# A list schedule made by the program orders units 0 to 7, the weight conversion and block 0 on four engines

## The chip, the cores and the metric

The kernel runs on one core of one Trainium2 chip. The metric is the device time of one execution in microseconds (us). A core has a matrix engine (TensorE, PE in the rows), whose weight loads are shown apart (PEld), and VectorE (DVE), ScalarE (ACT), GpSimd (POOL) and SyncE (SP), which here only issues DMA transfers. Each engine runs its own queue in order and waits on semaphores for the others. Matrix products are written to PSUM, of which the kernel uses eight banks of 512 columns; GpSimd can't read PSUM.

## What is computed

Linear attention is followed by a gated feed-forward layer and by a layer of eight experts with routing by the largest logit:

```python
def phi(x):                      # q, k: (4, 8, 576, 64)
    proj = einsum('bhsd,df->bhsf', x, w_phi)
    proj = proj - max(abs(proj), axis=-1)
    return concatenate([exp(proj), exp(-proj)], axis=-1)
kv, z = einsum('bhsf,bhsd->bhfd', phi(k), v), phi(k).sum(2)
attn = einsum('bhsf,bhfd->bhsd', phi(q), kv) / (einsum('bhsf,bhf->bhs', phi(q), z) + 1e-6)
x = attn as (2304, 512)
x = ((silu(x @ w_gate) * (x @ w_val)) @ w_out)        # 512 -> 1536 -> 512
# per token: the expert e of the largest gate logit; out = weights * relu(x @ w1[e]) @ w2[e]
```

## The kernel before

**Units.** The attention is cut into 16 units u of one batch and two heads. A unit has five kinds of steps. `step_qk` (three, c = 0 to 2) projects keys and queries on TensorE, takes a row maximum and subtracts it on VectorE, and makes the key exponentials on ScalarE; the query part is subtracted on VectorE, or for odd units below 8 on ScalarE with a bias. `step_kv` multiplies keys and values, and ScalarE copies the result. `step_tq` (three) transposes the queries, and ScalarE makes their exponentials. `step_num` makes numerator and denominator, and VectorE normalises them into `XT`. `step_tx` (two) transposes the output; ScalarE writes it rounded (`XH`), VectorE the rest (`XL`). Four units make 576 rows of the feed-forward's input.

**Weights.** They come as 64-bit words, 36 pieces (f, w) of 512 columns: column f = 0 to 11, w = gate, value or output weight. For each, SyncE loads a piece into one of three buffers (`conv_load`), ScalarE scales the upper words (L395) and rounds the lower ones (L397), VectorE makes a mask and a shift (L400, L401), GpSimd adds (L404). This is the conversion. Each use of a weight is split into a rounded part (`WH`, ScalarE, L434) and the rest (`WL`, GpSimd, L435), four buffers deep.

**Blocks.** The feed-forward runs over six blocks n of 384 rows. In a block, each column f has two projections of 12 matmuls (`mm_gv`, L444 to L448), a gate (`act_g`, `act_v`: tanh on ScalarE, two products and the rest `GL` on VectorE, L454 to L460), and an output product of 9 matmuls (`mm_o`, L468 to L470) one column later. Block 0 needs units 0 to 3, and it is the one that needs each weight freshly converted. Units 4 to 7 run beside block 0, units 8 to 15 beside blocks 1 to 3.

**What sets the order.** Up to `mark["fixed"]` the program writes TensorE's order out by hand: projections of units 0 and 1, then unit by unit, with some warm-up matmuls (`warmup`, L324) put between. The rest, and the other engines everywhere, are ordered by the framework's scheduler from the order in which the program records them: `run_to` and `conv_to` spread the steps of units 4 to 7 and the conversion evenly over block 0 (`pace`, 36 places), and `hold` keeps conversions from running over two columns ahead. Units in this stretch take turns on PSUM banks 0 to 6, from `mark[PROL - 1]` on banks 5 to 7.

## Time and profile before

| | before |
|---|---|
| median of 3 runs | 955.44 us (955.03 to 956.55) |
| the profiled execution | 956.69 us, span 954.7 us |
| busy PE, PEld | 910.9 us (95%), 791.5 us (83%) |
| busy DVE, ACT, POOL | 625.3 us (65%), 577.3 us (60%), 378.9 us (40%) |
| mean granted TensorE clock | 0.983 of full speed |
| first matmul of block 0, of block 1 | 68.17 us, 201.39 us |

The span runs from the first to the last instruction of the core; the execution's own time is 1.99 us longer. Busy time is the time in which at least one instruction of the engine is in flight. A share over the whole span is an average over stages with different limits, so the stages are read apart.

### The profile page before, as it was taken

Reading aid. Unit: us, or ns where it says so; the run is one execution under the profiler, and the core shown is the slowest. Engines: PE = TensorE matmul, PEld = TensorE weight load, DVE = VectorE, ACT = ScalarE, POOL = GpSimd, SP = SyncE. Lnnn points to the kernel's source line nnn. Section 1 sums busy time; section 2 is a strip of 40 time slices with the busy share of each in tenths; the row PEclk is TensorE's granted clock in tenths of the full one; section 3 lists DMA queues with packets and bytes.
Section 4 is the critical chain, followed back from the end, with each engine's and each line's share of the span. In section 5 each row is a group of like instructions: output and inputs, shape, how many; then the busy total and the mean of one; then the engine's idle time right before and its main releaser. Section 6 shows DMA issues by size and latency. Waiting matters only on the chain.

```text
span 954.7 us, 18339 instructions
## 1 busy us (share of the span) xinstructions
PE 910.9 (95%) x7136; PEld 791.5 (83%) x7136; DVE 625.3 (65%) x1106; ACT 577.3 (60%) x1028; POOL 378.9 (40%) x303
## 2 busy tenths in 40 slices
PE   8789888999999999999999999989999999999995
PEld 5678677799999888888989999979887888878874
DVE  6697787845453743556454543465599988898974
ACT  6876566654435445445545444444588998888873
POOL 1435665644544344434435566556201111112210
PEclk9999899999999999999999999989999999999998
DMA  9663353110001101120000000054001137165230
GB/s 269 170 196 102 126 172 128 46 58 16 1 14 61 26 16 40 26 73 15 1 2 22 14 1 1 34 214 173 34 23 45 45 133 292 40 235 194 98 139 11
DMA packets 20939, 78.88 MB, mean 83 GB/s; under 512 B 5358, under 2 KB 5614, under 8 KB 19056
## 3 DMA queue, kind: packets, MB, share of 16 engines
q1 hardware_dynamic: 17280, 67.60, 21.5%
q0 software_dynamic: 3200, 9.48, 3.0%
q8 instruction: 58, 0.95, 0.4%
q10 hardware_dynamic: 368, 0.59, 0.2%
q14 instruction: 33, 0.27, 0.1%
HBM read 123.23 MB, written 10.00 MB: 140 GB/s over the span
## 4 chain that ended last, share of the span: by engine, by line
PE 72%; issue 4%; DVE 4%; DMA 2%; ACT 1%; POOL 1%; POOLq 0%; DVEq 0%; ACTq 0%
PE banks L444 10%; PE banks L700 9%; PE banks L448 9%; PE banks L447 9%; PE banks L468 5%; PE banks L469 5%; PE banks L470 5%; PE banks L722 3%; PE banks L723 3%; PE banks L724 3%; PE banks L189 2%; PE banks L268 2%; PE banks L236 2%; PE banks L711 1%; DVE arena L483 1%
## 5 line engine op out<-in xcount | busy, mean ns | idle before, releaser
L435 POOL TENSOR_TENSOR arena_r<-arena,arena_r 128x512 fp32r<-128x512 f32 x216 | 284.5, 1319 | 266.9 <-ACT arena_r L434 244.6
L434 ACT ACTIVATE arena_r<-arena 128x512 fp32r<-128x512 f32 x216 | 136.6, 632 | 236.7 <-PE banks L447 146.1
L444 PE MATMUL banks<-arena_r 128*128 128x384 f32 x576 | 202.6, 352 | 0.0
L666 DVE TENSOR_TENSOR arena_r<-arena,arena_r 128x1024 fp32r<-128x1024 f32 x160 | 189.6, 1234 | 19.0 <-ACT arena_r L665 17.8
L448 PE MATMUL banks<-arena_r 128*128 128x384 f32 x576 | 193.7, 336 | 0.0
L447 PE MATMUL banks<-arena_r 128*128 128x384 f32 x576 | 193.4, 336 | 0.0
L665 ACT ACTIVATE arena_r<-arena 128x1024 fp32r<-128x1024 f32 x160 | 161.9, 1066 | 15.5 <-PE banks L700 10.9
L454 DVE SCALAR_TENSOR_TENSOR arena<-arena,banks 128x384 f32<-128x384 f32 x72 | 39.8, 552 | 120.7 <-ACT arena L453 120.4
L700 PE MATMUL banks<-arena_r 128*128 128x512 f32 x480 | 117.8, 398 | 0.0
L444 PEld LDWEIGHTS banks<-arena_r 128*128 128x128 f32 x576 | 108.4, 188 | 5.5 <-DVE arena L454 0.4
L447 PEld LDWEIGHTS banks<-arena_r 128*128 128x128 f32 x576 | 108.6, 189 | 1.2
L728 POOL DMA_INDIRECT out_dram<-arena x20 | 20.8, 1040 | 222.1 <-ACT arena L727 217.4
L448 PEld LDWEIGHTS banks<-arena_r 128*128 128x128 f32 x576 | 108.3, 188 | 0.0
L700 PEld LDWEIGHTS banks<-arena_r 128*128 128x128 f32 x480 | 88.9, 189 | 20.4 <-ACT arena_r L692 2.1
L460 DVE TENSOR_TENSOR arena_r<-arena,arena_r 128x384 fp32r<-128x384 f32 x72 | 70.4, 977 | 38.4 <-ACT arena_r L459 38.1
L468 PE MATMUL banks<-arena_r 128*128 128x512 f32 x216 | 90.5, 419 | 0.0
L469 PE MATMUL banks<-arena_r 128*128 128x512 f32 x216 | 86.9, 402 | 0.0
L470 PE MATMUL banks<-arena_r 128*128 128x512 f32 x216 | 86.6, 402 | 0.0
L722 PE MATMUL banks<-arena_r 128*128 128x512 f32 x160 | 62.7, 392 | 1.0 <-ACT arena_r L665 0.7
L457 DVE TENSOR_TENSOR arena<-arena,banks 128x384 f32<-128x384 f32 x72 | 39.7, 551 | 36.3 <-PE banks L448 36.1
L723 PE MATMUL banks<-arena_r 128*128 128x512 f32 x160 | 62.4, 390 | 0.0
L724 PE MATMUL banks<-arena_r 128*128 128x512 f32 x160 | 62.4, 390 | 0.0
(124 smaller groups left out, 1391.3 us busy)
## 6 DMA issues: line engine op xcount, KB each, us to landing
arena<-mw SPq DMA_DIRECT2D x40, 2048.0 KB
ov_conv<-w1cat SPq DMA_DIRECT2D x24, 512.0 KB
arena<-w1cat SPq DMA_DIRECT2D x12, 512.0 KB
arena<-v SPq DMA_DIRECT2D x16, 325.0 KB
x2d<-arena SPq DMA_DIRECT2D x18, 256.0 KB
arena<-qT SPq DMA_DIRECT2D x15, 288.0 KB
arena<-kT SPq DMA_DIRECT2D x15, 288.0 KB
ov_gather<-x2d,arena POOLq DMA_INDIRECT x20, 3.5
```

Source lines behind the costliest of these rows:

```text
L434: ACT.activation(wh, wr, AF.Copy)
L435: POOL.tensor_tensor(out=wl, in0=wr, in1=wh.bitcast(F32), op=ALU.subtract)
L444: mm = PE.matmul(ps, wh[:, c], xh, start=(k == 0), stop=False)
L447: PE.matmul(ps, wh[:, c], xl, start=False, stop=False)
L448: PE.matmul(ps, wl[:, c], xh, start=False, stop=(k == 3))
L468: PE.matmul(ps, GH[f % 2][:, ts_], woh, start=(f == 0), stop=False)
L469: PE.matmul(ps, GH[f % 2][:, ts_], wol, start=False, stop=False)
L470: PE.matmul(ps, GL[f % 2][:, ts_], woh, start=False, stop=(f == NFT - 1))
L665: ACT.activation(h, src, AF.Copy)
L666: DVE.tensor_tensor(out=l, in0=src, in1=h.bitcast(F32), op=ALU.subtract)
L700: PE.matmul(PS[:, HB[h], :], lhs, w[:, h * 512:(h + 1) * 512], start=a, stop=b)
L722: PE.matmul(ps, HTH[:, k, :], wh[:, cs], start=(k == 0), stop=False)
```

## The change

A class `Plan` takes operations with an engine, a duration in us, a due time and what they read and write. Its `run` simulates four engines (SyncE and the transfers as further ones) while the program is built: again and again it takes, of the operations whose inputs are done, the one that can start first, and among those of that engine which could start at the same time the one that is due first; it gives out PSUM banks, and calls the operation's function, so that the instructions are recorded in that order. `first_part` puts units 0 to 7, unit 8's projections, the 36 conversions, the splits and block 0 into it. The steps are cut into the part of each engine for that (`qk_mm`, `k_sub`, `k_exp`, `q_sub`, and so on). Where TensorE would stand idle for over 0.9 us in the plan before its time 56, `filler` puts warm-up matmuls. The order so made is fixed for PE, DVE, ACT and POOL.

Besides, the rounding of the first `NRP` = 8 pieces moves from ScalarE to GpSimd, the subtraction `g_lo` of block 0 from VectorE to GpSimd, the second output transpose is of 128 rows instead of 64 in its last part, and `hold` goes. Blocks 1 to 5 and units 8 to 15 are recorded as before.

```diff
-PRE = 9
 PROL = 4
-AHEAD = 2
+NRP = 8
 WARM = 11
...
+class Plan:
+    LAT = 0.15
+    def __init__(self):
+        self.ops, self.last_w, self.readers = [], {}, {}
+    def op(self, eng, dur, due, fn, reads=(), writes=(), banks=0, pool=(), holder=None):
+        i = len(self.ops)
+        deps = set()
+        for r in reads:
+            if r in self.last_w:
+                deps.add(self.last_w[r])
+            self.readers.setdefault(r, []).append(i)
+        for w in writes:
+            if w in self.last_w:
+                deps.add(self.last_w[w])
+            deps.update(self.readers.pop(w, ()))
+            self.last_w[w] = i
+        deps.discard(i)
+        if banks:
+            holder = {"users": 0, "end": 0.0, "owner": i}
+        elif holder is not None:
+            deps.add(holder["owner"])
+            holder["users"] += 1
+        self.ops.append(dict(eng=eng, dur=dur, due=due, fn=fn, deps=deps, banks=banks, pool=pool, holder=holder))
+        return holder
+    def run(self, filler):
+        ops = self.ops
+        left = [len(o["deps"]) for o in ops]
+        after = [[] for _ in ops]
+        for i, o in enumerate(ops):
+            for d in o["deps"]:
+                after[d].append(i)
+        end = [0.0] * len(ops)
+        free = {}
+        bank_free = [0.0] * 8
+        ready = {i for i, n in enumerate(left) if n == 0}
+        while ready:
+            best = None
+            for i in ready:
+                o = ops[i]
+                t = max([free.get(o["eng"], 0.0)] + [end[d] + self.LAT * (ops[d]["eng"] != o["eng"]) for d in o["deps"]])
+                if o["banks"]:
+                    b = sorted((bank_free[b], b) for b in o["pool"])[:o["banks"]]
+                    if b[-1][0] == float("inf"):
+                        continue
+                    t = max(t, b[-1][0] + self.LAT)
+                    o["take"] = [x[1] for x in b]
+                cand = (t, o["due"], i)
+                o["at"] = t
+                if best is None or cand < best:
+                    best = cand
+            assert best is not None, "no op can be taken"
+            same = [(ops[i]["due"], i) for i in ready if ops[i]["eng"] == ops[best[2]]["eng"]
+                    and ops[i].get("at", 1e9) <= best[0] + 0.05 and (not ops[i]["banks"] or all(
+                        bank_free[b] < float("inf") for b in ops[i].get("take", ())))]
+            i = min(same)[1]
+            o = ops[i]
+            ready.discard(i)
+            filler(o["eng"], free.get(o["eng"], 0.0), o["at"])
+            if o["banks"]:
+                o["holder"]["ps"] = [b for b in o["take"]]
+                for b in o["take"]:
+                    bank_free[b] = float("inf")
+                o["fn"](*o["take"])
+            elif o["holder"] is not None:
+                o["fn"](*o["holder"]["ps"])
+            else:
+                o["fn"]()
+            end[i] = o["at"] + o["dur"]
+            free[o["eng"]] = end[i]
+            h = o["holder"]
+            if h is not None and not o["banks"]:
+                h["users"] -= 1
+                h["end"] = max(h["end"], end[i])
+                if h["users"] == 0:
+                    for b in h["ps"]:
+                        bank_free[b] = h["end"]
+            for j in after[i]:
+                left[j] -= 1
+                if left[j] == 0:
+                    ready.add(j)
+        assert not any(left)
+        return free
...
-    for x in qk(0) + qk(1):
-        add(*x)
-    add(warmup, 6)
-    for u in range(PROL):
-        add(step_kv, u)
-        if u >= 2:
-            tx(u - 2)
-        for c in range(3):
-            add(step_tq, u, c)
-        if u:
-            add(step_num, u - 1)
-        add(warmup, 2)
-        for x in qk(u + 2) if u + 2 < PROL else []:
-            add(*x)
-    for x in qk(PROL):
-        add(*x)
-    tx(PROL - 2)
-    add(step_num, PROL - 1)
-    mark["fixed"] = len(steps)
-    tx(PROL - 1)
-    for u in range(PROL, 16):
-        if u == QSW:
-            add(step_ov)
+            PE.matmul(PS[:, 4, :], warm[:, 0:P], warm, start=True, stop=True)
+    add(step_ov)
+    for u in range(QSW, 16):
...
-        at = seen.get(i // 3 - AHEAD)
-        if at is not None:
-            tc.add_manual_dep(ins.ins, at.name, mybir.DependencyInfo(
-                mybir.DependencyClass.NoSync, mybir.DependencyReason.SCHED_ONLY), reason="pace of the weights")
...
+    def conv_round(i):
+        lo = ST[i % 3].rearrange("p (n two) -> p n two", two=2)[:, :, 0].bitcast(U32)
+        r = CP[i % 2].bitcast(I32)
+        if i < NRP:
+            POOL.tensor_scalar(out=r, in0=lo, scalar1=2.0 ** -29, scalar2=None, op0=ALU.mult)
+        else:
+            ACT.activation(r, lo, AF.Copy, scale=2.0 ** -29)
...
+    def g_lo(f, eng=DVE):
+        eng.tensor_tensor(out=GL[f % 2], in0=GP, in1=GH[f % 2].bitcast(F32), op=ALU.subtract)
...
+    def first_part():
+        pl = Plan()
+        op = pl.op
+        def unit(u, qkd, kvd, numd, txd):
+            z, early = two(u), u < PROL
+            sub = u % 2 == 0
+            banks = (0, 1, 2, 3, 5, 6, 7) if u < 3 else (0, 1, 2, 5, 6, 7) if u == 3 else (5, 6, 7)
+            for c in range(3):
+                d = qkd + 1.2 * c
+                h = op("PE", 0.8, d, lambda bq, bk, c=c: qk_mm(u, c, bq, bk), [("x", u)], [("qk", u, c), ("xr", u % 2)], 2, banks)
+                op("DVE", 1.1, d + 1, lambda bq, bk, c=c: k_sub(u, c, bk), [("qk", u, c)], [("kp", z, c)], holder=h)
+                op("ACT", 1.08, d + 2, lambda c=c: k_exp(u, c), [], [("kp", z, c)])
+                if sub:
+                    op("DVE", 1.1, d + 2, lambda bq, bk, c=c: q_sub(u, c, bq), [("qk", u, c)], [("tq", z, c)], holder=h)
+                else:
+                    op("DVE", 0.55, d + 2, lambda bq, bk, c=c: amax(bq, MQ[c]), [("qk", u, c)], [("m", c)], holder=h)
+                    op("ACT", 1.11, d + 3, lambda bq, bk, c=c: q_bias(u, c, bq), [("m", c)], [("tq", z, c)], holder=h)
+            if u >= 8:
+                return
+            h = op("PE", 2.2, kvd, lambda b: kv_mm(u, b), [("kp", z, c) for c in range(3)] + [("v", u)],
+                   [("kvm", u)], 1, banks)
+            op("ACT", 0.41, kvd + 1, lambda b: kv_copy(u, b), [("kvm", u)], [("kv", u % 2)], holder=h)
+            for c in range(3):
+                h = op("PE", 0.4, kvd + 1 + c, lambda b, c=c: tq_mm(u, c, b), [("tq", z, c)], [("tqm", u, c)], 1, banks)
+                op("ACT", 1.07, kvd + 2 + c, lambda b, c=c: tq_exp(u, c, b), [("tqm", u, c)], [("qp", z, c)], holder=h)
+            h = op("PE", 2.2, numd, lambda b0, b1: num_mm(u, b0, b1), [("qp", z, c) for c in range(3)] + [("kv", u % 2)],
+                   [("num", u)], 2, banks)
+            op("DVE", 1.36, numd + 1, lambda b0, b1: normalise(0, b0), [("num", u)], [("xt", 0), ("xt", 1)], holder=h)
+            op("DVE", 1.0, numd + 1.5, lambda b0, b1: normalise(1, b1), [("num", u)], [("xt", 0), ("xt", 1)], holder=h)
+            for part in range(2):
+                n = len(x_pieces(u, part))
+                js = sorted({x[1] for x in x_pieces(u, part)})
+                h = op("PE", 0.45, txd + part, lambda b, part=part: tx_mm(u, part, b), [("xt", part)],
+                       [("txm", u, part)], 1, banks)
+                op("ACT", 0.38 * n, txd + part + 0.5, lambda b, part=part: x_hi(u, part, b), [("txm", u, part)],
+                   [("xh", j, u) for j in js], holder=h)
+                op("DVE", 0.42 * n, txd + part + 0.7, lambda b, part=part: x_lo(u, part, b),
+                   [("txm", u, part)] + [("xh", j, u) for j in js], [("xl", j, u) for j in js], holder=h)
+        start = {("x", 0): 7.0, ("x", 1): 10.5, ("v", 0): 12.5, ("v", 1): 16.0, ("x", 2): 17.0, ("x", 3): 21.0}
+        start.update({("v", u): 0.0 for u in range(2, 8)})
+        for name, t in start.items():
+            op(("at",) + name, t, t, lambda: None, [], [name])
+        for u in range(4):
+            b = 7 + 11 * u
+            unit(u, b, b + 8, b + 13, b + 17)
+        B0, PER = 56.0, 9.6
+        for u in range(4, 9):
+            b = 48 + 28 * (u - 4)
+            unit(u, b, b + 10, b + 16, b + 21)
+        for i in range(3 * NFT):
+            f, w = divmod(i, 3)
+            due = B0 + PER * f + (0, 2, 6)[w] - 14
+            if i >= 3:
+                op("SP", 0.1, due - 8, lambda i=i: conv_load(i), [], [("st", i % 3)])
+                op(("dma", i), 4.0, due - 8, lambda: None, [], [("st", i % 3)])
+            else:
+                op(("dma", i), 14.0 + 3 * i, due - 8, lambda: None, [], [("st", i % 3)])
+            op("ACT", 0.69, due, lambda i=i: conv_scale(i), [("st", i % 3)], [("cu", i % 2)])
+            op("POOL" if i < NRP else "ACT", 1.65 if i < NRP else 0.69, due + 0.5, lambda i=i: conv_round(i), [("st", i % 3)], [("cp", i % 2)])
+            op("DVE", 1.75, due + 1, lambda i=i: conv_bits(i), [("cu", i % 2)], [("wr", i)])
+            op("POOL", 1.37, due + 3, lambda i=i: conv_add(i), [("cp", i % 2)], [("wr", i)])
+        last = where[1, 0, 0] + 2
+        def cut_weights(i):
+            n, f, w = uses[i]
+            due = B0 + PER * (12 * n + f + (1 if w == 2 else 0)) + (0, 3, 6)[w] - 5
+            op("ACT", 0.64, due, lambda: split_hi(i), [("wr", 3 * f + w)], [("wh", i % 4)])
+            op("POOL", 1.37, due + 1, lambda: split_lo(i), [("wh", i % 4), ("wr", 3 * f + w)], [("wl", i % 4)])
+        for i in range(3):
+            cut_weights(i)
+        for i in range(where[1, 0, 0]):
+            n, f, w = uses[i]
+            at = B0 + PER * (f + (1 if w == 2 else 0)) + (0, 3, 6)[w]
+            wts = [("wh", i % 4), ("wl", i % 4)]
+            xs = [(x, 0, u) for x in ("xh", "xl") for u in range(4)]
+            if w == 2:
+                op("PE", 2.1, at, lambda f=f: o_mm(0, f), wts + [("gh", f % 2), ("gl", f % 2)], [("out",)])
+            elif w == 0:
+                op("PE", 2.2, at, lambda f=f: gv_mm(0, f, 0), wts + xs, [("G",)])
+                op("ACT", 0.49, at + 1, g_tanh, [("G",)], [("ts",)])
+                op("DVE", 0.55, at + 1.5, g_mul, [("ts",), ("G",)], [("gp",)])
+            else:
+                op("PE", 2.2, at, lambda f=f: gv_mm(0, f, 1), wts + xs, [("V",)])
+                op("DVE", 0.55, at + 1, v_mul, [("V",)], [("gp",)])
+                op("ACT", 0.53, at + 1.5, lambda f=f: g_hi(f), [("gp",)], [("gh", f % 2)])
+                op("POOL", 1.05, at + 2, lambda f=f: g_lo(f, POOL), [("gp",), ("gh", f % 2)], [("gl", f % 2)])
+            cut_weights(i + 3)
+        def filler(eng, t0, t1):
+            if eng == "PE" and t1 < B0 and t1 - t0 > 0.9:
+                warmup(int((t1 - t0 - 0.3) / 0.4))
+        ET = mybir.EngineType
+        with tc.manual_schedule(engines={ET.PE, ET.DVE, ET.Activation, ET.Pool}):
+            ends = pl.run(filler)
...
-    with tc.manual_schedule(engines={mybir.EngineType.PE}):
-        for i in range(mark["fixed"]):
-            run_to(i + 1)
-            conv_to(PRE * 3 * i // mark["fixed"])
-    run_to(mark[PROL - 1])
+    POOL.memset(XT[64:P, 4, :], 0.0)
+    first_part()
     state["banks"] = [5, 6, 7]
-    need = {0: mark[7], 1: mark[8] - 2, 2: mark[11], 3: mark[15], 4: 0, 5: 0}
-    for i in range(3):
-        split(i)
-    prev = None
+    need = {1: mark[8] - 2, 2: mark[11], 3: mark[15], 4: 0, 5: 0}
+    prev = (0, NFT - 1)
```

**What moves, on TensorE at the start.** In both orders the rows below are the steps of unit 0 behind its projections (128x512 is a warm-up; 64x130 and 64x65 are kv; 128x128 x9 or x3 query transposes). Before, ahead of them stand 11 warm-ups, the 36 projections of units 0 and 1, and 6 warm-ups:

```order
L227 MATMUL banks<-arena 64x130 x4
L236 MATMUL banks<-arena 64x65 x32
L248 MATMUL banks<-arena 128x128 x9
L324 LDWEIGHTS arena
L324 MATMUL banks<-arena 128x512
```

After, ahead of the rows below stand 28 warm-ups; the first row with x18 is unit 0's projections, the rows with x6 are unit 1's:

```order
L459 MATMUL banks<-arena 128x512
L286 MATMUL banks<-arena 128x128 x18
L365 MATMUL banks<-arena 128x128 x3
L286 MATMUL banks<-arena 128x128 x6
L459 LDWEIGHTS arena
```

The transposes of unit 0 have moved ahead of unit 1's projections, one chunk at a time. Before block 0 there are 20 more warm-ups in eight places, where there were 14.

**On VectorE around the first gate of block 0.** Before (L400 and L401 are a conversion, L454, L457 and L460 the gate, L310 is `XL` of unit 3):

```order
L400 TENSOR_SCALAR arena<-arena 128x512
L310 TENSOR_TENSOR arena_r<-banks,arena_r 128x384
L310 TENSOR_TENSOR arena_r<-banks,arena_r 128x192
L401 SCALAR_TENSOR_TENSOR arena<-arena 128x512
L400 TENSOR_SCALAR arena<-arena 128x512
L454 SCALAR_TENSOR_TENSOR arena<-arena,banks 128x384
L401 SCALAR_TENSOR_TENSOR arena<-arena 128x512
L457 TENSOR_TENSOR arena<-arena,banks 128x384
L460 TENSOR_TENSOR arena_r<-arena,arena_r 128x384
```

After (L504 and L505 are the conversion, L552 and L555 the gate, L440 is `XL`):

```order
L440 TENSOR_TENSOR arena_r<-banks,arena_r 128x384
L440 TENSOR_TENSOR arena_r<-banks,arena_r 128x192
L504 TENSOR_SCALAR arena<-arena 128x512
L505 SCALAR_TENSOR_TENSOR arena<-arena 128x512
L504 TENSOR_SCALAR arena<-arena 128x512
L505 SCALAR_TENSOR_TENSOR arena<-arena 128x512
L552 SCALAR_TENSOR_TENSOR arena<-arena,banks 128x384
L504 TENSOR_SCALAR arena<-arena 128x512
L505 SCALAR_TENSOR_TENSOR arena<-arena 128x512
L555 TENSOR_TENSOR arena<-arena,banks 128x384
```

The third operation of the gate has left VectorE, and the conversions stand whole. Six conversions stand before unit 3's last `XL`, 30 behind it; 12 had been done by 68 us before.

**On GpSimd at the same place.** Before (L404 adds of the conversion, L435 splits):

```order
L435 TENSOR_TENSOR arena_r<-arena,arena_r 128x512 x3
L404 TENSOR_TENSOR arena<-arena,ov_conv 128x512
L435 TENSOR_TENSOR arena_r<-arena,arena_r 128x512
L404 TENSOR_TENSOR arena<-arena 128x512
L435 TENSOR_TENSOR arena_r<-arena,arena_r 128x512
```

After (L509 adds, L526 splits, L498 the last rounding on GpSimd, L561 `g_lo` of columns 0 and 1):

```order
L498 TENSOR_SCALAR arena<-ov_conv 128x512
L509 TENSOR_TENSOR arena<-arena,ov_conv 128x512
L509 TENSOR_TENSOR arena<-arena 128x512
L526 TENSOR_TENSOR arena_r<-arena,arena_r 128x512
L509 TENSOR_TENSOR arena<-arena,ov_conv 128x512
L561 TENSOR_TENSOR arena_r<-arena,arena_r 128x384
L526 TENSOR_TENSOR arena_r<-arena,arena_r 128x512
L509 TENSOR_TENSOR arena<-arena 128x512
L526 TENSOR_TENSOR arena_r<-arena,arena_r 128x512
L561 TENSOR_TENSOR arena_r<-arena,arena_r 128x384
```

Eight roundings now stand on GpSimd ahead of block 0, and from there on a `g_lo` in each column among the adds and splits.

## Rows read from the trace of the kernel before

**Rows 1.** Windows: us, busy PE, PEld, DVE, ACT, POOL, PEclk, DMA share, GB/s.

```profile
0.00:68.17 68.17, 56.23 (x920) 44.47 (x920) 52.78 (x121) 50.77 (x119) 20.62 (x23) 0.95 0.75 218
68.17:201.39 133.22, 119.31 (x1083) 103.18 (x1082) 101.69 (x175) 83.97 (x183) 79.72 (x59) 0.96 0.36 109
201.39:300.00 98.61, 98.61 (x765) 90.02 (x765) 45.58 (x93) 46.51 (x92) 51.61 (x40) 1.00 0.08 26
```

**Rows 2.** TensorE's waits up to 200 us: us in total, times, longest.

```profile
PE banks L189 <- DVE arena L207: 5.2, 4, 2.9
```

**Rows 3.** Timeline of PE: start, us, line, operation, shapes, count; idle before.

```profile
1.20 4.88 PE L324 MATMUL banks<-arena 128*128 128x512 bf16 x11 [1.20 <-DVE arena L771]
6.00 3.05 PE L189 MATMUL banks<-arena 64*128 64x128 f32 x38
...
20.60 0.59 PE L324 MATMUL banks<-arena 128*128 128x512 bf16 x2
21.12 2.28 PE L189 MATMUL banks<-arena 64*128 64x128 f32 x36
...
26.92 1.15 PE L268 MATMUL banks<-arena 128*64 128x65 f32 x32
...
29.38 0.60 PE L324 MATMUL banks<-arena 128*128 128x512 bf16 x2
...
49.06 0.55 PE L297 MATMUL banks<-arena 128*128 128x128 f32 x3
...
49.85 1.20 PE L248 MATMUL banks<-arena 128*128 128x128 f32 x9
```

**Rows 4.** Timeline of PE where block 1 starts.

```profile
201.39 0.44 PE L444 MATMUL banks<-arena_r 128*128 128x384 f32 x1
...
205.68 0.39 PE L468 MATMUL banks<-arena_r 128*128 128x512 f32 x1
...
207.75 0.60 PE L499 MATMUL banks<-arena 128*128 128x128 f32 x4
```

**Rows 5.** Timeline of DVE at the start.

```profile
7.53 1.02 DVE L197 TENSOR_REDUCE arena<-banks 128x3 f32<-128x384 f32 x2 [6.39 <-PE banks L189]
...
9.40 1.01 DVE L197 TENSOR_REDUCE arena<-banks 128x3 f32<-128x384 f32 x2
```

**Rows 6.** DVE by line up to 206 us: count | busy us, mean ns | idle before.

```profile
L401 DVE SCALAR_TENSOR_TENSOR arena<-arena 128x512 int32<-128x512 int32 x36 | 34.5, 959 | 0.9
L400 DVE TENSOR_SCALAR arena<-arena 128x512 int32<-128x512 int32 x36 | 29.0, 805 | 6.2 <-ACT arena L395 4.7
...
L460 DVE TENSOR_TENSOR arena_r<-arena,arena_r 128x384 fp32r<-128x384 f32 x12 | 11.2, 932 | 12.1 <-ACT arena_r L459 12.0
...
L310 DVE TENSOR_TENSOR arena_r<-banks,arena_r 128x192 fp32r<-128x192 f32 x16 | 5.5, 352 | 2.4 <-ACT arena_r L309 2.3
...
L310 DVE TENSOR_TENSOR arena_r<-banks,arena_r 128x384 fp32r<-128x384 f32 x4 | 2.2, 556 | 1.8 <-ACT arena_r L309 1.8
```

**Rows 7.** Timeline of DVE, the normalisation of unit 5.

```profile
121.10 0.17 DVE L276 TENSOR_SCALAR arena<-banks 128x6 f32<-128x6 f32 x1 [2.65 <-PE banks L265]
...
122.75 0.86 DVE L280 TENSOR_TENSOR arena<-banks,arena 64x256 f32<-64x256 f32 x2
```

**Rows 8.** Timeline of DVE, two conversions.

```profile
123.84 0.43 DVE L400 TENSOR_SCALAR arena<-arena 128x512 int32<-128x512 int32 x1 [0.23 <-ACT arena L395]
124.30 0.69 DVE L401 SCALAR_TENSOR_TENSOR arena<-arena 128x512 int32<-128x512 int32 x1
125.10 1.56 DVE L400 TENSOR_SCALAR arena<-arena 128x512 int32<-128x512 int32 x1
126.69 1.66 DVE L401 SCALAR_TENSOR_TENSOR arena<-arena 128x512 int32<-128x512 int32 x1
```

**Rows 9.** Timeline of POOL in the same us.

```profile
125.07 1.30 POOL L404 TENSOR_TENSOR arena<-arena 128x512 int32<-128x512 int32 x1 [2.51 <-DVE arena L401]
126.32 1.48 POOL L435 TENSOR_TENSOR arena_r<-arena,arena_r 128x512 fp32r<-128x512 f32 x1
```

249 lines of the change are left out of this document (132 added, 117 removed).

## Prediction

> **What bounds the kernel now.** The busy time by stage comes first, because the share over the whole span (TensorE 95%) hides where it is lost. From the first matmul of block 1 at 201.39 us on [rows 4], TensorE is busy for 98.61 of 98.61 us; before that it has two stages with holes: 56.23 busy of 68.17 us up to the first matmul of block 0, and 119.31 of 133.22 us in block 0 [rows 1]. I call them stage A and stage B. Since TensorE has no idle time behind 201.39, what the first part saves reaches the end one to one, and the change touches the first part alone. So the question is: when does block 1 start after the change?
>
> The view of waits says what the holes are: TensorE waits for VectorE and ScalarE to hand over the small steps of a unit, 5.2 us in four waits for a `q_sub` alone [rows 2]. No engine is full over both stages: VectorE is busy for 52.78 + 101.69 us, ScalarE 50.77 + 83.97, GpSimd 20.62 + 79.72 of 201.39 [rows 1]. TensorE's 119.31 busy us in stage B also contain work at the lower clock, whose granted mean there is 0.96 [rows 1].
>
> **How much TensorE must do.** In an undisturbed run of instructions a unit's projections, kv, query transposes and num steps take from 21.12 to 29.38 us, 8.26 us, and its output transposes 49.06 to 49.85, 0.79 us: 9.05 us a unit; without num and output transposes 5.8 us (21.12 to 26.92) [rows 3]. A weight column f costs 4.29 us for its two projections (201.39 to 205.68) and 2.07 us for its output product (205.68 to 207.75) [rows 4].
>
> **The change, part by part, stage A.** The list of TensorE's order has 28 warm-up matmuls ahead of the first unit where there were 11, and 20 more before block 0 where there were 14. The 11 take from 1.20 to 6.00 us, 0.44 us each; the two behind unit 0 go at 0.26 us (20.60 to 21.12) [rows 3]. The 17 new ones cost 4.4 us at the one pace and 7.5 at the other; I take 5.1 (the first four at the slow pace), because data of unit 0 are there by 6.00. So the projections start at 11.1 us, and VectorE, which starts at 7.53 now [rows 5], at 12.6.
>
> VectorE then has, up to the last `x_lo` of unit 3: 54 maxima and subtractions, at 0.47 us each (four from 7.53 to 9.40, [rows 5]) 25.4 us; six weight conversions at 0.805 + 0.959 = 1.76 us, 10.6 us [rows 6] (the old order has 12 by then); four normalisations of 2.5 us (121.10 to 123.61, [rows 7]), 10.0 us; four `x_lo` of 0.96 us (7.7 us for eight units, [rows 6]), 3.9 us. That is 49.9 us, and 62.5 us is the earliest end. TensorE's own work up to there is four units at 9.05, 5.8 for the fifth and 20 fillers at 0.26: 47.2 us, end at 58.3. So VectorE leads stage A. Today it is busy for 52.78 of the 60.6 us from 7.53 to 68.17, 87%; at that rate the stage would end at 69.9. I take 64: the list hands each engine its steps one at a time and interleaved, the three transposes of a query chunk right behind its subtraction, and 1.76 us already contains waits.
>
> **Stage B.** TensorE: twelve columns at 4.29 and eleven output products at 2.07 us (the twelfth lies in block 1 in both orders), 74.3 us; num and output transposes of unit 4, 3.25; units 5 to 7, 27.2; one of unit 8's three projection steps, 0.76. Sum 105.4 us. Two steps of unit 8, 1.5 us, slip behind the start of block 1; today none does. VectorE: 30 conversions at 1.76, 52.8; 24 gate products at 0.47, 11.3; 34 maxima and subtractions, 16.0; four normalisations and `x_lo`, 13.9: 94.0 us. Its twelve `g_lo` (932 ns, [rows 6]) go to GpSimd, and eight of ScalarE's roundings of weights with them, in stage A; ScalarE only gets lighter and had 49 us free in stage B [rows 1].
>
> GpSimd is where the price is. The rows at 125 us show a DVE conversion and a GpSimd operation that exclude each other: the mask of a conversion takes 0.43 and its shift 0.69 us alone (123.84, 124.30), but 1.56 and 1.66 us against GpSimd operations [rows 8], each ending 0.29 and 0.55 us after GpSimd's at 126.37 and 127.80 [rows 9]. VectorE's operations on PSUM are not stretched: `x_lo` of 384 columns has a mean of 0.556 us [rows 6]. So the two queues share one resource. In stage B it has to carry 27 conversion adds and 32 splits at 1.25 us (125.07 to 126.32), 73.8 us; eleven `g_lo` on GpSimd, which no row shows: 0.94 us by the length, 384 of 512 columns, 10.3 us (bounds: 0.56 us, a subtraction of this size on VectorE, and 1.5, a held GpSimd operation; 6 to 16 us in all); and 30 conversions at 0.29 + 0.55, 25.2 us, or 33.6 at the lengths they have alone. Sum 109.3 to 117.7 us: more than TensorE's 105.4, and no list that leaves this resource out can see it. The eight roundings on GpSimd are not in the trace either; between 1.25 and 2.5 us (twice the other operation) they are 10 to 20 us of stage A, where GpSimd is idle for 47.5 of 68.17 us, so they cost nothing unless they delay a conversion.
>
> The Trainium skill says the same of the resource (GPSIMD Engine Reference, Key points): GpSimd shares its SBUF interfaces with VectorE, and contends with DVE instructions in a two-port mode or with two SBUF inputs; the rows agree (1.66 against 0.69 us). Its section Engine selection speaks against `g_lo` on GpSimd: two-input elementwise work is about twice as slow there; as an estimate by that, 1.1 us each and 1.8 us more over the eleven.
>
> Stage B lies between 109.3 us (the shared resource never idle) and the 133.2 of today. I take 120, near the middle: the resource would then be used for 91% of the stage, VectorE for 78% (76% today) and TensorE for 88% at the full pace, against 105.4 / 133.2 = 79% today.
>
> **The sum.** Block 1 starts at 64 + 120 = 184 us in place of 201.39; less the 1.5 us that slip, 15.9 us are saved. The profiled execution took 956.69 us for a span of 954.70; its span should become about 938.8. The median of the runs is 955.44, 1.25 below that execution; 15.9 less gives 939.5 us.
>
> **Rivals.** *The list is kept nearly as planned.* Nothing waits but for the shared resource: block 1 at 62.5 + 109.3 = 171.8, saved 28.1, 927.3 us; with TensorE alone as the bound 167.9 and 923.4 us. For it: VectorE reached 87% in stage A already. Against it: the exclusion, which stretches both queues when both are busy. Chance 0.15.
>
> *Little is gained.* The late start stays (stage A ends at 69.9, VectorE at 87%), and stage B takes 126 us, since each of four fixed orders waits for the others where they run late: block 1 at 195.9, saved 4.0, 951.4 us. For it: with fixed orders on four engines one late step holds everything behind it, a `split_hi` on ScalarE that waits for TensorE to free a weight buffer, for example. Chance 0.13; another 0.06 that it comes out within 0.2%.
>
> *The alternation of VectorE and GpSimd, slower.* With GpSimd's queue never empty, every conversion meets an operation there twice and takes 1.56 + 1.66 = 3.22 us, as at 125.10 [rows 8]. 30 times 1.46 us more makes 137.8 us of VectorE's 94.0; filled to 97%, stage B takes 142 us, block 1 starts at 206, and the kernel takes 955.44 + 4.6 + 1.5 = 961.5 us. It decides from 3.02 us a conversion on (131.8 us of VectorE in 135.9). Against it: GpSimd is busy for 84 of 120 us, not always, and many DVE operations lie between two conversions. Chance 0.08.
>
> **Numbers.** The forecast (932 to 948 us) has 0.58, the four others 0.15, 0.13, 0.06 and 0.08. About 0.2%, 1.9 us, is what a measurement of this kernel can tell from no change. Faster: 0.58 + 0.15 + 0.13 = 0.86; within: 0.06; slower: 0.08. The range must reach into the first two rivals: 927 leaves out the part of the first that TensorE alone bounds, 953 the last two cases; together about 0.2.
>
> **What the profile after would show.** First projection near 11 us; first matmul of block 0 near 64; first of block 1 near 184; TensorE full behind it as now. The mean of mask and shift together should be 1.7 to 2.2 us; above 3 the third rival is right, below 1.5 the exclusion was overrated. `g_lo` on GpSimd near 0.94 us. If TensorE's idle time in stage B is under 5 us, the first rival holds; if block 0 starts after 68, stage A was misjudged, and the warm-ups or VectorE's waits say why. The prediction is wrong if TensorE behind block 1 shows holes it has not now, since the whole argument rests on there being none.

## The result, and the profile after

| | before | after |
|---|---|---|
| median (range) | 956.00 us (955.03 to 958.07) | 945.78 us (945.33 to 946.96) |
| ratio, 95% interval | | 0.9892 [0.9873, 0.9912] |
| the profiled execution, its span | 956.69, 954.7 us | 945.33, 943.6 us |
| first projection | 6.00 us | 9.04 us |
| first matmul of block 0 (stage A) | 68.17 us | 64.31 us |
| first matmul of block 1 | 201.39 us | 190.73 us |
| block 0 (stage B) | 133.22 us | 126.42 us |

The kernel became 10.2 us faster. Block 1 starts 10.66 us earlier and the span is 11.1 us shorter, so the first part alone made the difference, nearly one to one. The forecast had 15.9 us.

The three windows of the kernel after answer to [rows 1] (us, then busy PE, PEld, DVE, ACT, POOL with instructions, PEclk, DMA share, GB/s):

```profile
0.00:64.31 64.31, 58.44 (x942) 45.54 (x942) 48.10 (x109) 42.97 (x101) 23.29 (x25) 0.97 0.64 182
64.31:190.73 126.42, 114.56 (x1063) 99.60 (x1062) 110.14 (x166) 89.78 (x190) 103.19 (x79) 0.97 0.47 136
190.73:290.00 99.27, 98.85 (x736) 89.62 (x737) 50.51 (x102) 47.64 (x95) 50.25 (x39) 1.00 0.09 27
```

Stage A came out at 64.31 us. From block 1 on TensorE is nearly full (98.85 of 99.27 us), as it was before. Stage B is 6.4 us longer than the 120 forecast. In it TensorE is idle for 11.86 us, but no engine is full over the whole stage: VectorE has 87%, GpSimd 82%, with 79 instructions where it had 59.

The waits of TensorE in stage B (us in total, times, longest) answer to [rows 2]:

```profile
PE banks L542 <- POOL arena_r L526: 4.5, 3, 3.0
PE banks L286 <- DVE arena_r L440: 2.5, 2, 2.1
PE banks L422 <- DVE arena L407: 2.3, 1, 2.3
PE banks L540 <- DVE arena L552: 1.0, 1, 1.0
PE banks L365 <- DVE arena L309: 0.7, 1, 0.7
```

L542 is the part of a column's projections that uses `WL`, and L526 the split that makes it; L440 writes `x_lo`, L407 is the normalisation, L309 a `q_sub`. TensorE now waits for GpSimd and VectorE, in few and long waits, and one short one is for a `q_sub`.

Before, the subtraction of a query was the largest cause of its waits: 7.7 us up to 200 us for a `q_sub` on VectorE (L207, 5.2 us in [rows 2] and the 2.5 below), and 9.6 us for the same step with a bias on ScalarE (L205):

```profile
PE banks L189 <- ACT arena L205: 3.5, 1, 3.5
...
PE banks L300 <- DVE arena L207: 2.5, 2, 1.6
PE banks L297 <- ACT arena L205: 2.4, 1, 2.4
PE banks L300 <- ACT arena L205: 2.2, 2, 1.2
...
PE banks L248 <- ACT arena L205: 1.5, 2, 0.7
```

Of these 17.3 us, the kernel after has 4.5 left: the 0.7 in stage B, and in stage A

```profile
PE banks L365 <- DVE arena L309: 2.5, 4, 1.2
PE banks L286 <- ACT arena L314: 1.3, 1, 1.3
```

By line, the mask (L504) and the shift (L505) of the conversion in stage B answer to [rows 6] (busy us, mean ns, idle before):

```profile
L505 DVE SCALAR_TENSOR_TENSOR arena<-arena 128x512 int32<-128x512 int32 x31 | 40.7, 1313 | 1.1
L504 DVE TENSOR_SCALAR arena<-arena 128x512 int32<-128x512 int32 x30 | 29.9, 998 | 3.2 <-ACT arena L491 2.4
```

Together 2.31 us a conversion, against the 1.76 taken. That 1.76 is a mean over both stages of the kernel before. In its stage B alone, where GpSimd was busy for 60%, the two took 1.93 us, and in its stage A 1.41 (485 and 927 ns):

```profile
L401 DVE SCALAR_TENSOR_TENSOR arena<-arena 128x512 int32<-128x512 int32 x25 | 24.1, 964 | 0.6
L400 DVE TENSOR_SCALAR arena<-arena 128x512 int32<-128x512 int32 x24 | 23.2, 965 | 4.4 <-ACT arena L395 3.3
```

In stage A of the kernel after, where GpSimd is busy for 23.29 of 64.31 us, they take 0.91 and 0.52 us:

```profile
L505 DVE SCALAR_TENSOR_TENSOR arena<-arena 128x512 int32<-128x512 int32 x6 | 5.5, 911 | 0.2
...
L504 DVE TENSOR_SCALAR arena<-arena 128x512 int32<-128x512 int32 x6 | 3.1, 517 | 0.1
```

GpSimd's own lines in stage B, splits (L526) and the moved `g_lo` (L561):

```profile
L526 POOL TENSOR_TENSOR arena_r<-arena,arena_r 128x512 fp32r<-128x512 f32 x35 | 49.5, 1420 | 5.2 <-ACT arena_r L522 4.0 <-issue 1.2
...
L561 POOL TENSOR_TENSOR arena_r<-arena,arena_r 128x384 fp32r<-128x384 f32 x12 | 14.3, 1189 | 2.1 <-ACT arena_r L558 2.1
```

What stretches the conversion is seen in six us of the timelines of VectorE and GpSimd (start, us); they answer to [rows 8, 9]:

```profile
136.69 1.55 DVE L504 TENSOR_SCALAR arena<-arena 128x512 int32<-128x512 int32 x1
138.27 1.39 DVE L505 SCALAR_TENSOR_TENSOR arena<-arena 128x512 int32<-128x512 int32 x1
139.58 0.55 DVE L294 TENSOR_REDUCE arena<-banks 128x3 f32<-128x384 f32 x1
140.04 1.32 DVE L504 TENSOR_SCALAR arena<-arena 128x512 int32<-128x512 int32 x1
141.40 1.68 DVE L505 SCALAR_TENSOR_TENSOR arena<-arena 128x512 int32<-128x512 int32 x1
```

```profile
136.66 1.29 POOL L509 TENSOR_TENSOR arena<-arena,ov_conv 128x512 int32<-128x512 int32 x1 [0.63 <-DVE arena L505]
137.91 1.20 POOL L561 TENSOR_TENSOR arena_r<-arena,arena_r 128x384 fp32r<-128x384 f32 x1
139.80 1.28 POOL L509 TENSOR_TENSOR arena<-arena 128x512 int32<-128x512 int32 x1 [0.69 <-DVE arena L505]
141.04 1.49 POOL L526 TENSOR_TENSOR arena_r<-arena,arena_r 128x512 fp32r<-128x512 f32 x1
```

The mask at 136.69 starts 0.03 us behind an add and ends at 138.24, 0.29 us after it (137.95); the shift at 138.27 starts inside the `g_lo` that ends at 139.11 and ends 0.55 us after it. Alone they take 0.43 and 0.69 us. The reduction from PSUM at 139.58 takes its usual 0.55.

### The profile page after: what moved, and what is told of

The parts are those of the page before. It is cut to its first block, busy times and chain, and to the rows that moved or that the text cites. A ratio compares the mean times of both kernels' runs of the same rounds, so it can differ in the third digit from the quotient of the medians.

```text
span 943.6 us, 18408 instructions
## 1 busy us (share of the span) xinstructions
PE 908.5 (96%) x7159; PEld 790.2 (84%) x7159; DVE 640.8 (68%) x1094; ACT 578.2 (61%) x1020; POOL 404.6 (43%) x324
## 4 chain that ended last, share of the span: by engine, by line
PE 76%; DVE 15%; issue 4%; DMA 3%; ACT 2%; POOL 0%; POOLq 0%; DVEq 0%; ACTq 0%
PE banks L915 10%; PE banks L540 10%; PE banks L542 9%; PE banks L541 9%; PE banks L578 5%; PE banks L579 5%; PE banks L580 5%; PE banks L286 3%; DVE arena L505 3%; PE banks L937 3%; PE banks L938 3%; PE banks L939 3%; DVE arena L504 2%; PE banks L347 2%; PE banks L390 2%
## 5 line engine op out<-in xcount | busy, mean ns | idle before, releaser
L526 POOL TENSOR_TENSOR arena_r<-arena,arena_r 128x512 fp32r<-128x512 f32 x216 | 285.8, 1325 | 247.2 <-ACT arena_r L522 234.4
L542 PE MATMUL banks<-arena_r 128*128 128x384 f32 x576 | 193.9, 337 | 4.5 <-POOL arena_r L526 4.5
L915 PE MATMUL banks<-arena_r 128*128 128x512 f32 x480 | 116.8, 396 | 0.0
L540 PEld LDWEIGHTS banks<-arena_r 128*128 128x128 f32 x576 | 108.3, 188 | 7.8 <-issue 1.4
L542 PEld LDWEIGHTS banks<-arena_r 128*128 128x128 f32 x576 | 108.1, 188 | 5.8 <-POOL arena_r L526 5.8
L552 DVE SCALAR_TENSOR_TENSOR arena<-arena,banks 128x384 f32<-128x384 f32 x72 | 39.7, 552 | 107.6 <-ACT arena L549 107.5
L578 PE MATMUL banks<-arena_r 128*128 128x512 f32 x216 | 90.0, 417 | 0.0
L579 PE MATMUL banks<-arena_r 128*128 128x512 f32 x216 | 86.6, 401 | 0.0
L580 PE MATMUL banks<-arena_r 128*128 128x512 f32 x216 | 86.5, 402 | 0.0
L561 DVE TENSOR_TENSOR arena_r<-arena,arena_r 128x384 fp32r<-128x384 f32 x60 | 60.9, 1015 | 27.7 <-ACT arena_r L558 27.5
L294 DVE TENSOR_REDUCE arena<-banks 128x3 f32<-128x384 f32 x96 | 52.7, 554 | 23.6 <-PE banks L286 21.5
L555 DVE TENSOR_TENSOR arena<-arena,banks 128x384 f32<-128x384 f32 x72 | 39.8, 552 | 39.6 <-PE banks L542 38.8
L937 PE MATMUL banks<-arena_r 128*128 128x512 f32 x160 | 62.7, 392 | 1.0 <-ACT arena_r L880 0.7
L939 PE MATMUL banks<-arena_r 128*128 128x512 f32 x160 | 62.4, 390 | 0.0
```

The lines of the kernel that those rows point to most:

```text
L526: POOL.tensor_tensor(out=WL[i % 4], in0=WR[f][w], in1=WH[i % 4].bitcast(F32), op=ALU.subtract)
L540: PE.matmul(ps, wh[:, c], xh, start=(k == 0), stop=False)
L542: PE.matmul(ps, wl[:, c], xh, start=False, stop=(k == 3))
L578: PE.matmul(ps, GH[f % 2][:, ts_], woh, start=(f == 0), stop=False)
L579: PE.matmul(ps, GH[f % 2][:, ts_], wol, start=False, stop=False)
L580: PE.matmul(ps, GL[f % 2][:, ts_], woh, start=False, stop=(f == NFT - 1))
```

## The experiments

The first theory after the result was **VectorE alone**: its work in stage B, 94.0 us by the forecast, grew by 30 x 0.55 = 16.5 to 110.5, and it shows 110.14. The rivals were **the shared resource** of the prediction (GpSimd's operations and VectorE's conversions exclude each other, so their sum counts), and that the order itself leaves holes. Stage A ends at the first matmul of block 0, stage B at that of block 1. Where a run gives an operation another engine, length or due time in the plan, the program makes its list anew, so the order of the whole first part differs too: this is so in e1, e5, e6, e7, e8 and e10. e3, e4 and e11 keep the order of the kernel after on VectorE, ScalarE and GpSimd.

**Which part of the change gains.** e7 keeps the planner and puts `g_lo` and the roundings back; e9 keeps the old order and moves only these two to GpSimd.

```diff
 e7_order_only, against the kernel after
-NRP = 8
+NRP = 0
-op("POOL", 1.05, at + 2, lambda f=f: g_lo(f, POOL), ...
+op("DVE", 0.98, at + 2, lambda f=f: g_lo(f), ...
 e9_place_only, against the kernel before
-            ACT.activation(ri, st[:, :, 0].bitcast(U32), AF.Copy, scale=2.0 ** -29)
+            if i < 8:
+                POOL.tensor_scalar(out=ri, in0=..., scalar1=2.0 ** -29, scalar2=None, op0=ALU.mult)
+            else: ACT.activation(...)
-        DVE.tensor_tensor(out=GL[f % 2], ...)
+        (POOL if n == 0 else DVE).tensor_tensor(out=GL[f % 2], ...)
```

Expected of e7: 

> The list's order without the two moves: g_lo on VectorE and all roundings on ScalarE. Theory now (the resource that GpSimd and VectorE's two conversion operations share is the bound of stage B, not VectorE alone): the roundings lie in stage A, where GpSimd is idle for 41 of 64 us, so nothing changes against the run with g_lo alone moved back: 937 to 941 us. Rival (ScalarE needs the relief in stage A): stage A 3 to 5 us longer, 942 to 944 us.

Expected of e9: 

> The old order and the old scheduler with the two moves alone: g_lo of block 0 and the first eight roundings on GpSimd. If the moves are worth something by themselves (11 us of VectorE and 5.5 of ScalarE less): 948 to 952 us. Theory (the moves only load the shared resource, which the old order does not fill): 954 to 958 us. If an output product waits for g_lo behind other work on GpSimd: over 959 us.

| | old placement | `g_lo`, roundings on GpSimd |
|---|---|---|
| old order | 955.93 us | e9: 957.52 us, 1.0016 [1.0002, 1.0029] |
| new order | e7: 941.09 us, 0.9835 [0.9817, 0.9854] | after: 945.78 us, 0.9892 [0.9873, 0.9912] |

The order gains 11.7 to 14.8 us, and the two placements together cost 1.6 us in the old order and 4.7 in the new one. (The small changes beside the order, the transpose of 128 rows and the missing `hold`, are in e7 too and were not tried apart.) Stages A and B of e7 are 72.12 and 118.11 us, of e9 71.80 and 134.83. e9 came out as the theory had it. e7 did not: against e1 below, which has only `g_lo` put back, its stage A is 7.8 us longer, as its rival said and by more, and its stage B 3.4 us shorter, with two conversions fewer (28 for 30). The stage A of e7 also has more matmuls (1009 for 941) and a lower granted clock (0.91 for 0.97), so why it is longer stays open. All the same, the roundings on GpSimd show no cost: with them block 1 starts 4.4 us earlier (185.81 for 190.24), and the median is 2.2 us lower, though the ranges overlap. By these runs the loss of the placements is `g_lo`'s.

**What `g_lo` on GpSimd costs.** e1 is the kernel after with `g_lo` alone back on VectorE (its second `-`/`+` pair above). Expected: 

> Undoes one part: g_lo of block 0 is back on VectorE, in the plan with 0.98 us. Theory (exclusion: stage B is 126.4 us in place of 120 because a conversion on VectorE meets GpSimd operations and takes 2.31 us in place of 1.76): VectorE, 87% busy in stage B and 96% from 110 to 170 us, gets 11 operations of about 1.1 us, and its 60 conversion operations wait some 4 us less; stage B 6 to 8 us longer, 951 to 954 us. Rival (the four fixed orders wait for each other, and no engine is the bound): 944 to 948 us.

Measured: 938.85 us, 0.9828 [0.9807, 0.9848], below both ranges. Stage A is unchanged (64.34). The window of stage B and, in it, VectorE's lines:

```profile
64.34:185.81 121.47, 113.75 (x1076) 99.08 (x1074) 112.96 (x185) 91.39 (x193) 88.32 (x66) 0.99 0.48 141
```

```profile
L505 DVE SCALAR_TENSOR_TENSOR arena<-arena 128x512 int32<-128x512 int32 x31 | 35.4, 1141 | 1.1
L504 DVE TENSOR_SCALAR arena<-arena 128x512 int32<-128x512 int32 x30 | 27.0, 901 | 3.1 <-ACT arena L491 3.0
...
L561 DVE TENSOR_TENSOR arena_r<-arena,arena_r 128x384 fp32r<-128x384 f32 x12 | 9.9, 826 | 0.0
```

VectorE got twelve more operations and is busier (112.96 us of 121.47), and the stage is 4.95 us shorter. That fells the theory that VectorE's own work is the bound. The conversion fell from 2.31 to 2.04 us, which pays 8.1 of the 9.9 us that `g_lo` takes there. How much of the 4.95 us is the place of `g_lo` and how much the new list, this run can't tell; e11 below keeps the list.

**How little of GpSimd's work must stay for the holes to close.** In e3 GpSimd's operations of the first part work on 32 columns in place of 512 or 384; the rest of the low parts of weights and gates is left out. With that the routing is another and the expert layer runs more slots, so its total, 1011.64 us (1.0581 [1.0557, 1.0605]), is not to be compared; stages A and B issue the same instructions.

```diff
-        POOL.tensor_tensor(out=WL[i % 4], in0=WR[f][w], ...)
+        POOL.tensor_tensor(out=WL[i % 4][:, 0:c], in0=WR[f][w][:, 0:c], ...)
 (c = 32; and so for the rounding, the add and g_lo)
```

Expected: 

> Leaves out 15 of 16 columns (11 of 12 for g_lo) of every GpSimd operation in stages A and B, so that most of the low parts of the weights stay unset; all instructions, waits and orders stay. Theory (exclusion): mask and shift take 1.15 us together in place of 2.31, VectorE in stage B falls from 110 us to about 75, and TensorE's own 105 us are the bound: stage B 106 to 112 us, 926 to 932 us in all. Rival (fixed orders waiting for each other): TensorE's waits stay, 942 to 946 us; between them, 933 to 941, both have a share.

The window of stage B, and its two lines of the conversion:

```profile
63.65:171.79 108.14, 108.09 (x1063) 97.06 (x1061) 75.76 (x165) 88.02 (x190) 22.59 (x78) 1.00 0.52 157
```

```profile
L505 DVE SCALAR_TENSOR_TENSOR arena<-arena 128x512 int32<-128x512 int32 x30 | 20.9, 696 | 1.0
L504 DVE TENSOR_SCALAR arena<-arena 128x512 int32<-128x512 int32 x30 | 13.1, 437 | 7.3 <-ACT arena L491 6.6
```

The same order, with nearly the same number of instructions on every engine, leaves TensorE no wait at all: 108.09 busy of 108.14 us, at the full clock. So the order has no holes of its own, and TensorE's work in stage B is 108.1 us (105.4 forecast). The conversion takes 1.13 us, the sum of its lengths alone (0.43 and 0.69). VectorE's list of operations is the same, only GpSimd's operations are shorter: this shows that what GpSimd does is what stretches the conversion.

**`g_lo` where it is, but short.** e11 cuts only `g_lo` to 32 columns, on GpSimd, at its place; the low part of block 0's gates is zero in the other 352. It tells the hold of a `g_lo` from its place in the queue.

```diff
-        eng.tensor_tensor(out=GL[f % 2], in0=GP, ...)
+        c = 32 if eng is POOL else BT
+        eng.tensor_tensor(out=GL[f % 2][:, 0:c], in0=GP[:, 0:c], ...)
```

Expected: 

> The changed kernel with the g_lo of block 0 left on GpSimd, at the same place of its queue, but 32 columns wide instead of 384; this leaves out 352 columns of the low part of the gates of block 0, which is zero there. It measures what g_lo holds of the resource that GpSimd and VectorE share. Shared-resource theory: a g_lo shrinks from 1.19 to about 0.3 us, twelve of them give back 8 to 11 us, stage B takes 115 to 119 us (e1, where VectorE has them at half the hold, 121.5), and the mean of mask and shift falls below 2.1 us together. Rival, the hand-over: what e1 gained is g_lo's place (late on GpSimd, behind splits, with the output product behind it): then the thin g_lo in the same place keeps most of the loss, stage B 124 to 126.5. Rival, length only: g_lo is only shorter by 0.9 us on a queue that is not full, and stage B gains as much as the waits of TensorE on GpSimd end (4.5 us of waits on a split): 122 us. The total may be read only if blocks 1 to 5 keep their length; the stages decide.

Measured: 942.20 us, 0.9854 [0.9834, 0.9875]; its stage A is 1.7 us longer than after's (the first projection starts at 10.10 us for 9.04). Window of stage B and lines:

```profile
66.01:187.63 121.62, 112.67 (x1063) 98.61 (x1062) 104.14 (x166) 89.30 (x190) 93.94 (x79) 0.99 0.49 142
```

```profile
L505 DVE SCALAR_TENSOR_TENSOR arena<-arena 128x512 int32<-128x512 int32 x31 | 34.4, 1108 | 1.1
L504 DVE TENSOR_SCALAR arena<-arena 128x512 int32<-128x512 int32 x30 | 30.4, 1015 | 3.9 <-ACT arena L491 3.1
```

```profile
L562 POOL TENSOR_TENSOR arena_r<-arena,arena_r 128x32 fp32r<-128x32 f32 x12 | 6.0, 499 | 2.2 <-ACT arena_r L558 2.2
```

The place alone, the hand-over rival, falls: stage B is 4.8 us shorter with `g_lo` in its old place. But the shared resource had 115 to 119 us, and 121.62 is what the third rival (length on GpSimd) had. A thin `g_lo` takes 0.50 us, not 0.3, and gives back 12 x 0.69 = 8.3 us, of which the stage shows 4.8. So the sum of the resource has the sign right, and near TensorE's 108 us it no longer gives its size. This run can't tell which of the two queues a `g_lo` held back.

**A plan that knows the exclusion.** In e6 the simulated queues of GpSimd and of the conversions exclude each other, with the lengths that the operations have alone; the work is the same.

```diff
+                if o["excl"]:
+                    t = max(t, port)
...
+            if o["excl"]:
+                port = end[i]
-            op("DVE", 1.75, due + 1, lambda i=i: conv_bits(i), ...
+            op("DVE", 1.15, due + 1, lambda i=i: conv_bits(i), ..., excl=True)
```

Expected: 

> The changed kernel with another plan: a conversion's two VectorE operations (1.15 us) and all GpSimd operations (1.27, 1.53 and 1.0 us) can't overlap in it; which engine does what stays. Theory (the shared resource is the bound): it needs the same 96 + 25 = 121 us in stage B whatever the order, 941 to 946 us. Rival (the order is wrong because the plan gives a conversion 1.75 us and it takes 2.31): an order that knows of it loses less, stage B 113 to 118 us, 932 to 938 us.

Measured: 946.05 us, 0.9892 [0.9875, 0.9909], with A 70.52 and B 123.26. A better informed order of the same work gave nothing: stage B is 3.2 us shorter, stage A 6.2 longer, with two conversions more in A. And yet its conversions in stage B are much shorter than after's, 1.79 us for 2.31, with GpSimd busy for 76% of it:

```profile
L511 DVE SCALAR_TENSOR_TENSOR arena<-arena 128x512 int32<-128x512 int32 x28 | 28.1, 1002 | 1.0
L510 DVE TENSOR_SCALAR arena<-arena 128x512 int32<-128x512 int32 x28 | 22.1, 789 | 3.7 <-ACT arena L497 3.0
```

So an order that keeps the two apart makes VectorE's operations shorter (VectorE is busy for 96.54 of 123.26 us), but TensorE then waits for the splits instead (5.1 us in two waits on GpSimd's L532).

**Conversions earlier.** e5 lets them fall due 20 us earlier (`- 14` to `- 34` in their due time).

Expected: 

> Due times of the conversion 20 us earlier: 13 conversions on VectorE stand before unit 3's last x_lo in place of 6. Theory (exclusion, and conversions in the wrong stage): in stage A VectorE is idle for 16 us and GpSimd for 41, so the seven cost 2 to 5 us there, and take 7 x 2.3 = 16 us of VectorE out of stage B, which falls to 113 to 117 us: 936 to 941 us. Rival (only the sum of VectorE's work counts): stage A gets longer by 7 x 1.76 = 12 us and stage B shorter by as much: 944 to 948 us.

Measured: 948.20 us, 0.9921 [0.9902, 0.9940]. Stage B is 7.9 us shorter (118.54), stage A 10.3 longer (74.58), much as the rival said (12 each way); the theory's 936 to 941 us failed. The new list also moves some 70 of TensorE's matmuls from B to A (992 in B for 1063), so the conversions' share isn't told apart. All of this work must be done before block 1 starts, wherever it lies.

**The warm-ups.** e4 leaves out the 17 new warm-ups ahead of the first unit.

```diff
-            if eng == "PE" and t1 < B0 and t1 - t0 > 0.9:
+            if eng == "PE" and t0 > 0 and t1 < B0 and t1 - t0 > 0.9:
```

Expected: 

> Undoes one part: the 17 warm-up matmuls that the plan puts ahead of unit 0 go, the rest of the plan stays. If stage A is a chain from the first projections: they start at about 6.1 us in place of 9.04, stage A ends 2 to 3 us earlier, and the kernel takes 943 us. Rival: the first projections then run at the lower clock, or the loads of units 1 to 3 are what stage A waits for: 945 to 947 us.

Measured: 942.94 us, 0.9867 [0.9847, 0.9888]. The first projection moves from 9.04 to 5.61 us, block 0 to 61.54, block 1 to 187.97, and stage B stays at 126.43. Its first window against after's:

```profile
0.00:61.54 61.54, 55.69 (x925) 44.60 (x925) 48.19 (x109) 42.73 (x101) 23.30 (x25) 0.97 0.67 188
```

VectorE's work is the same, the granted clock too (0.97), and 2.8 us are gone. So the 17 warm-ups delay: by 3.4 us at the first projection and 2.8 at block 0. The difference is about the 0.68 us that TensorE waits in e4 for the load of `q`, behind the first twelve projections.

**Together.** e10 is e1 and e4 in one. Expected: 

> The changed kernel with two parts undone: g_lo of block 0 on VectorE (planned at 0.98 us, as in e1_glo_dve), and no warm-up matmuls beyond 11 ahead of unit 0 (as in e4_start11). If the two act in different stages, their gains add: block 0 starts near 61.5 us (e4 61.54), stage B takes near 121.5 (e1 121.47), block 1 starts at 183, and the time is 938.9 - 2.8 = 936 us (934 to 938). If an earlier start only lets stage B run into the same limit sooner (a finish of the conversions that does not move, say), block 1 stays at 185.8 and the time at 938 to 940.

Measured: 935.02 us (934.46 to 935.84), 0.9789 [0.9772, 0.9805], the fastest of all. Block 0 starts at 61.90, block 1 at 182.56:

```profile
61.90:182.56 120.66, 112.89 (x1075) 97.76 (x1074) 112.78 (x185) 91.20 (x193) 88.33 (x66) 1.00 0.48 143
```

The gains add: e1 and e4 alone gain 6.9 and 2.8 us, both together 10.8. e8 has e6's plan besides, with `g_lo` on VectorE planned at 0.55 us. Expected: 

> That plan, with g_lo back on VectorE (0.55 us, also exclusive in the plan) and without the 17 warm-ups ahead of unit 0. Theory (shared resource): the sum of the parts, 938.9 less 2.8, 935 to 937 us. Rival (a plan that knows the exclusion orders better): another 3 to 6 us less, 930 to 933 us.

Measured: 938.77 us, 0.9826 [0.9805, 0.9847]; A 64.62, B 120.92. The median is 3.8 us behind e10's, and in the profiled executions block 1 starts 3.0 us later (185.54). The plan with the exclusion is the slower one here.

## Why the prediction was right, and what was mis-sized

**The frame held.** The change touches the first part alone, and what block 1 gains the end gains: 10.66 us of start, 11.1 of span, and TensorE nearly full behind it. The gain is the order's (e7, e9), and the waits that the prediction named are mostly gone: 17.3 us for the subtraction of a query became 4.5. The measured 945.78 us lies near the upper end of the forecast's 932 to 948; the gain was 10.2 us of the 15.9.

**Stage A: 64 forecast, 64.31 measured, by luck: errors cancel.** The 17 warm-ups cost 3.0 us (9.04 for 6.00; e4 gives 3.4 at the projection and 2.8 at block 0), not 5.1. From the first projection to block 0 it took 55.3 us, not 52.9. VectorE is busy for 48.10 us there, near the 49.9 worked out; six conversions at 1.43 us in place of 1.76 are 2.0 us less. What the 64 took too well is how full VectorE would be: 49.9 us from 12.6 to 64 are 97%. It starts at 10.11 and is busy for 47.8 of the 54.2 us up to block 0, 88%, as it was before (87%). The interleaved list did not fill it more; it had less to do and began earlier.

**Stage B: 120 forecast, 126.42 measured. This is where the prediction went wrong**, in the count of the shared resource and in one of its prices. The prediction gave GpSimd 27 adds and 32 splits, 59 operations. That is the number of its stage B before (25 adds and 34 splits); but with 30 conversions on VectorE in that stage, their adds come with them. After, there are 31 adds and 35 splits, and one rounding of 1.57 us. At the prediction's own 1.25 us these seven more are 8.8 us; twelve `g_lo` at 1.0 us (the shortest took 1.004, the mean is 1.189) instead of 10.3 for eleven are 1.7; with the rounding, 12.0 us. The sum is 109.3 + 12.0 = 121.3 us, in a stage of 126.42: the resource is used for 96% of it by this estimate, where the prediction took 91% (109.3 of 120). The lower end of its bounds was set 12 us too low. Its higher price, 33.6 us for the conversions at the lengths they have alone, would make the sum 129.7, more than the stage: as a hold of the resource that price is too high, by this estimate.

The same sum for the experiments, with 0.84 us a conversion as in the prediction, is an estimate: e1, 65 operations at 1.25, the rounding, 25.2, and twelve `g_lo` at 0.55 (as long as a subtraction of that size from PSUM) give 114.6 of 121.47 us, 94%; e11, with 12 x 0.3 for the thin ones (a thin split takes 0.30 in e3, an add 0.25 to 0.27), 112.9 of 121.62, 93%. In e3 GpSimd has 22.59 us, 47.8 with the conversions, and TensorE is the bound. In the lists made anew the sum explains less: e7 63 operations, 28 conversions and twelve `g_lo`, 108.9 of 118.11 us; e6 62, 28 and eleven, 112.0 of 123.26; e8 63, 28 and eleven, 108.3 of 120.92; e5 58, 22 and twelve, 103.0 of 118.54. So in the runs of the new order the stage is longer than the sum, outside e3 by 5 us (after) to 16 (e5): the sum is a lower bound in these runs, and not the length of the stage. e3 and e11, which keep the order, show that GpSimd's load, and not VectorE's own work, sets stage B; e1 agrees. That GpSimd stretches the conversions is shown by e3; that the sum of both is what limits the stage is argued from the timeline (ends 0.29 and 0.55 us after GpSimd's), and the amount that e11 missed stays open.

**The price of a conversion**, 1.7 to 2.2 us forecast, was 2.31. The 1.76 of [rows 6] was a mean over both stages before; the price in stage B alone could be read there, 1.93. With the lists of the scheduler and of the plain plan it rises roughly with GpSimd's share of the stage: 1.13 us at 21% (e3), 1.41 at 30% (stage A before), 1.43 at 36% (stage A after), 1.93 at 60% (before), 2.08 at 65% (e9), 2.04 at 73% (e1, e7), 2.12 at 77% (e11), 2.26 at 78% (e5), 2.31 at 82% (after). The order counts as well: in the lists that know the exclusion it is 1.79 at 76% (e6) and 1.75 at 71% (e8). It is no constant of the operation.

**`g_lo` on GpSimd**: 0.94 forecast in bounds of 0.56 to 1.5; measured 1.19 there, and 0.83 on VectorE (e1). The Trainium skill (GPSIMD Engine Reference, Engine selection) puts two-input elementwise work at about twice as slow on GpSimd, an estimate of 1.1 us: the mean agrees better with it than with the prediction's length rule, and the shortest, 1.004, lies between the two. The move costs 6.9 us (after against e1, whose list is made anew), 4.95 of them in stage B, more than the 1.8 that the estimate adds; the prediction's sum charged the move only to the resource and nothing to the conversions that a `g_lo` holds back (2.31 us for 2.04).

**The slip of two unit-8 steps**, 1.5 us, did not show as a loss: from block 1's start to the end it takes 752.87 us, before 753.31. Of the gap of 4.8 us between the forecast span (938.8) and the measured one (943.6), stages A and B have 0.3 and 6.4 against, this 1.9 for. That time differs between 749.86 (e8) and 754.38 us (e5) in runs whose code from block 1 on is the same, so a start of block 1 is worth itself at the end to about 2 us, and 1.5 us can't be told there.

**The rivals.** The list kept as planned is e3's case, and only with GpSimd nearly empty. "Little is gained" had stage B right at 126 us and stage A wrong at 69.9. The alternation, from 3.02 us a conversion on, didn't come: 2.31.

## What to carry to other kernels

When two queues exclude each other, count every operation of both in the new stage, the ones that come along with a moved step too, and take this sum as a lower bound: the share of each engine alone looked harmless here. Take a price from the stage that it is used for: the mean over both stages, 1.76 us, hid the 1.93 of the one that mattered. Moving an operation to an idler engine isn't free when the engines share something: ten microseconds of `g_lo` moved off VectorE cost five in the stage. A schedule made from measured durations takes them from one load and one order; where a duration depends on what the neighbour does (1.13 to 2.31 us here), they no longer hold in the order that it makes.
